# The values matmuls of half a head pair in one group, with the work of two other engines re-placed around it

## The chip, the cores and the metric

The kernel runs on one core of a Trainium2 chip. What counts is the device time of one launch in microseconds (us). The core has five engines that each run their own instructions in order: PE (TensorE, matmuls; its weight loads are listed apart as PEld), DVE (VectorE), ACT (ScalarE), POOL (GpSimd) and SP (SyncE, which issues most of the DMAs). They wait for each other by semaphores.

## The reference

The program is bucketed attention for 4 batches of 8 heads (768 positions, 64 channels a head), followed by a feed-forward layer with a rational function as its activation:

```python
mask = q_bucket[:, :, :, None] == k_bucket[:, :, None, :]   # bucket: the signs of 6 projections
scores = scale * np.matmul(q, k.transpose(0, 1, 3, 2))
scores = np.where(mask, scores, -1000000000.0)
scores = scores - np.max(scores, axis=-1, keepdims=True)
attn = np.exp(scores)
attn = attn / (np.sum(attn, axis=-1, keepdims=True) + 1e-09)
out = np.matmul(attn, v)
# then, on the tokens: h = x @ w_in;  g = P(h) / (Q(h) + 1e-6);  y = g @ w_out
```

All of it is in fp32. The fast matmul form takes numbers of fewer bits, so the kernel splits an operand into a rounded high part and the low rest, and multiplies the parts.

## The kernel before

**Attention, by head pairs.** Two heads make a pair, and there are 16 pairs. A pair has 12 steps `s`: two halves of the queries (`hf`, 384 columns each) by six tiles of 128 keys. One step is

- `scores`: for each of the two heads two matmuls (high parts with the mask rows, 76 or 77 rows deep; then the low parts, 128 deep) into one PSUM bank `pss`, and one Exp on ACT from that bank into an SBUF tile `E`; POOL adds the `E` tiles of three steps into an accumulator `acc` (two adds, one for each head, at each second and third step);
- `values`: for each head one matmul of `E` with the values `v` into the bank `psv` of that half, 64 columns of weights wide, the two heads beside each other. These are fp32 matmuls; each shows as two passes. After the sixth step `values_out` copies the bank out on ACT (`col`, then `xo`).

`sums` adds the accumulators over the partitions with eight narrow matmuls (32 columns of ones) into the bank `psu`, and ACT copies them to `sr`. So that Exp never overflows, each pair's largest scores are found beforehand: `maxstep` computes two matmuls into `psm` and DVE reduces them to a column of `m`, twelve times a pair, two pairs ahead. `shift_turn` turns the maxima by a matmul with the identity (`pst`, then `mt` on DVE).

**Preparation, beside it.** For a pair two ahead ACT rounds q and k to their high parts (`high`), DVE subtracts these from the originals (`low`, tiles `lo`), `bits` multiplies q and k with the projections (`psb`, 32 columns wide, for two pairs at once), DVE makes bucket rows `mb` of them, and ACT scales these (`penalties`). `weights` converts one of the 32 weight tiles every six steps, from 64-bit words: ACT takes both halves of a word (`ws`, `wr`), DVE masks, shifts and combines them (a TENSOR_SCALAR, a SCALAR_TENSOR_TENSOR and an add of integers, which the profile calls CUSTOM_DVE and the program order ISA), ACT rounds the result (`wi_hi`, or `wr` for w_out), and DVE subtracts (`wi_lo`, or `wr`). `recips` takes the reciprocals of the sums of a batch, after each fourth pair.

**What sets the order.** A plan by hand: `at(p, s, f)` puts the call `f` at time 12·p + s, and the calls are issued in the order of these numbers. Each engine keeps this order, so a number decides both which neighbours a call has on its engine and what stands behind it in the queue. Before, the values of a step are issued 1.3 to 2.3 steps after its scores, for two steps at a time (in pairs 0 and 15 for one), and `weights`, `low` and `high` stand at steps of their own among the scores. PSUM has eight banks: three rotate under the tag `s` (scores, transposes, sums), one holds `v`, and two double banks hold `psm` and `psb`. `E` has six buffers and `acc` six.

**After attention** come 128 steps of the feed-forward layer (`psh`, `pso`), from about 437 us to the end. All lines of the profile read L61, that of the helper that records the order; instructions are told apart by their tiles.

Of the kernel before, what the change touches and what calls it, by code (L numbers as in the profile page):

```python
# [17 lines left out]
P = 128  # L18
# [19 lines left out]
ACCS = 6  # L38
# [99 lines left out]
def attention(ctx, tc, nc, raw, ps_b, tail, tokens, early, operands_to_terms, ffn, load, QF, KF, v, w_in, w_out, wo_d, ident, cst, ones, prj,  # L138
# [15 lines left out]
    Q1, Q2, K1, K2, LO, V, M, MB, ACC, EXP, AV, MS = ({} for _ in range(12))  # L154
# [33 lines left out]
    def bits(p, which=(0, 1)):  # L188
# [5 lines left out]
        sl = slice(64 * which[0], 64 * which[-1] + 64)  # L194
# [31 lines left out]
    def shift_turn(p, hf=None):  # L226
# [4 lines left out]
        ps = ps_b.tile([P, 512], F32, tag="s", bufs=3, name=f"pst{p}_{hf}")  # L231
# [14 lines left out]
    def scores(p, s):  # L246
# [3 lines left out]
        for h in range(2):  # L250
            ps = ps_b.tile([P, 512], F32, tag="s", bufs=3, name=f"pss{p}_{s}_{h}")
# [31 lines left out]
    def sums(p):  # L283
        ps = ps_b.tile([P, 512], F32, tag="s", bufs=3, name=f"psu{p}")
# [33 lines left out]
    def weights(i):  # L318
# [13 lines left out]
        else:  # L332
# [34 lines left out]
    for p in range(NPAIR):  # L367
        for s in range(12):
# [17 lines left out]
        if p > 1:  # L386
            for t in range(2):
# [267 lines left out]
```

## Time and profile before

| what | value |
|---|---|
| median of 3 runs | 985.38 us (982.52 to 987.13) |
| the profiled execution | 982.12 us |
| its span, first to last instruction | 980.3 us |
| busy share of the span, PE / PEld / DVE / ACT / POOL | 98 / 76 / 85 / 69 / 45 % |
| attention, up to the first `psh` | about 437 us |

The page lists busy times, the span in 40 slices, the chain that ended last, and the costliest groups of instructions. In a row such as `PE MATMUL psv<-E,v 128*64 128x385` the tile written stands left of the arrow, the tiles read right of it, then the weights (rows*columns) and the streamed operand. In a timeline the columns are the start, the time from the first start to the last end, the engine, and how many instructions are merged; what is in brackets is the idle time before and what ended it.

### The profile page before, as it was taken

The page shows a single profiled execution, that of the slowest core. Times are in us where ns is not written, and L with a number is a line of the kernel's source. Part 1 is how long each engine was busy: PE and PEld are TensorE (multiplying, and loading weights), DVE is VectorE, ACT ScalarE, POOL GpSimd, SP SyncE. Part 2 cuts the span into 40 slices and gives each one's busy share as a digit, 9 for nine tenths or more (in the row PEclk, how much of TensorE's full clock was granted, in tenths as well). Part 3 has the DMA queues.
Part 4 walks back from the last instruction along what each step waited for, and adds up shares of the span by engine and source line. Part 5 has one row for each costly group of instructions (what it writes and reads, how often), then busy time and mean ns, then how long its engine had stood idle before and what let it go on. Part 6 is the DMA issues. An engine that isn't in the chain of part 4 may idle for free.

```text
span 980.3 us, 14803 instructions
## 1 busy us (share of the span) xinstructions
PE 957.6 (98%) x5009; PEld 744.8 (76%) x5009; DVE 835.4 (85%) x1200; ACT 679.2 (69%) x1411; POOL 436.8 (45%) x396
## 2 busy tenths in 40 slices
PE   5899999999999999999999999999999999999998
PEld 2556666666656666559999999999999999999996
DVE  5487778777877777568999999999999999999996
ACT  2356767676666666678777777777777777777775
POOL 1257776777677777782222222222222222222222
PEclk7699999999999999999999999999999999999999
DMA  7656676767686767737502111011011021110000
GB/s 202 175 169 185 184 201 171 202 186 198 183 254 211 242 190 206 236 126 260 169 1 66 33 49 48 1 65 33 1 65 33 1 65 33 62 36 1 33 1 32
DMA packets 50491, 112.97 MB, mean 115 GB/s; under 512 B 9296, under 2 KB 21968, under 8 KB 50416
## 3 DMA queue, kind: packets, MB, share of 16 engines
q1 hardware_dynamic: 49580, 110.59, 37.9%
q10 hardware_dynamic: 836, 1.44, 0.6%
q8 instruction: 39, 0.64, 0.3%
q14 instruction: 36, 0.29, 0.1%
HBM read 56.82 MB, written 21.17 MB: 80 GB/s over the span
## 4 chain that ended last, share of the span: by engine, by line
PE 92%; DVE 3%; DMA 3%; ACT 1%; SPq 0%; issue 0%; ACTq 0%; DVEq 0%
PE psh L61 27%; PE pso L61 27%; PE pss L61 15%; PE psv L61 13%; PE psm L61 6%; PE psu L61 2%; DVE m L61 1%; PE psb L61 1%; DMA wr<-w_out 1%; DMA q<-lo 0%; SPq L61 0%; DVE c L61 0%; DMA v<-v 0%; DMA prj<-proj 0%; DMA q<-mt 0%
## 5 line engine op out<-in xcount | busy, mean ns | idle before, releaser
L61 POOL TENSOR_TENSOR gl<-c,gh 128x384 fp32r<-128x384 f32 x128 | 140.4, 1097 | 395.4 <-ACT gh L61 368.8
L61 DVE TENSOR_REDUCE m<-psm 128x1 f32<-128x768 f32 x192 | 182.0, 952 | 92.5 <-PE psm L61 90.4
L61 PE MATMUL pso<-wo,gh 128*128 128x512 f32 x768 | 241.1, 395 | 0.0
L61 ACT ACTIVATE E<-pss 128x384 f32<-128x384 f32 x384 | 168.3, 492 | 79.7 <-PE pss L61 72.8
L61 POOL TENSOR_TENSOR acc<-E,E 128x384 f32<-128x384 f32 x128 | 150.9, 1199 | 113.9 <-ACT E L61 113.9
L61 PE MATMUL pss<-q,k 77*128 77x384 f32 (+1 forms) x768 | 180.2, 357 | 2.5 <-DMA q<-mt 1.5
L61 PEld LDWEIGHTS pss<-q,k 77*128 77x128 f32 (+1 forms) x768 | 134.0, 192 | 60.3 <-issue 50.1
L61 PE MATMUL psh<-xl,wi_hi 128*128 128x384 f32 x512 | 172.1, 336 | 0.0
L61 PE MATMUL psh<-xh,wi_hi 128*128 128x384 f32 x512 | 171.8, 336 | 0.0
L61 PE MATMUL psh<-xh,wi_lo 128*128 128x384 f32 x512 | 171.6, 335 | 0.0
L61 PEld LDWEIGHTS pso<-wo,gh 128*128 128x128 f32 x768 | 142.9, 188 | 23.7
L61 PE MATMUL pso<-wo,gl 128*128 128x512 f32 x384 | 152.3, 397 | 0.3 <-POOL gl L61 0.3
L61 ACT ACTIVATE h<-psh 128x384 f32<-128x384 f32 x128 | 62.9, 492 | 123.9 <-PE psh L61 123.9
L61 PE MATMUL psv<-E,v 128*64 128x385 f32 x768 | 148.3, 503 | 0.0
L61 DVE SCALAR_TENSOR_TENSOR c<-c,ab,r 128x384 f32<-128x384 f32 x128 | 146.9, 1147 | 0.0
L61 POOL TENSOR_TENSOR acc<-acc,E 128x384 f32<-128x384 f32 x128 | 142.7, 1135 | 7.8 <-ACT E L61 5.9
L61 PE MATMUL psm<-k,q 76*128 76x384 f32 x384 | 107.8, 365 | 7.0 <-DMA k<-mb 3.7
L61 PEld LDWEIGHTS psh<-xh,wi_hi 128*128 128x128 f32 x512 | 96.1, 188 | 6.3 <-ACT w L61 0.6
L61 PEld LDWEIGHTS psh<-xl,wi_hi 128*128 128x128 f32 x512 | 96.1, 188 | 5.1
L61 PEld LDWEIGHTS psh<-xh,wi_lo 128*128 128x128 f32 x512 | 96.2, 188 | 0.0
L61 PEld LDWEIGHTS psv<-E,v 128*64 128x64 f32 x768 | 45.7, 136 | 60.0 <-issue 52.4
L61 ACT ACTIVATE c<-psh,ab 128x384 f32<-128x384 f32 x128 | 86.5, 676 | 1.7 <-POOL gl L61 1.7
(62 smaller groups left out, 1233.8 us busy)
## 6 DMA issues: line engine op xcount, KB each, us to landing
q<-q SPq DMA_DIRECT2D x48, 192.0 KB
k<-k SPq DMA_DIRECT2D x48, 192.0 KB
wr<-w_in SPq DMA_DIRECT2D x16, 512.0 KB
wr<-w_out SPq DMA_DIRECT2D x16, 512.0 KB
wo_d<-wr SPq DMA_DIRECT2D x16, 512.0 KB
wo<-wo_d SPq DMA_DIRECT2D x16, 512.0 KB
q<-lo SPq DMA_DIRECT2D x32, 192.0 KB
k<-lo SPq DMA_DIRECT2D x32, 192.0 KB
```

Source lines behind the costliest of these rows:

```text
L61: return self.tc.keep_in_program_order(issue(*args, **kwargs))
```

## The change

- The values of a half are issued together: all twelve matmuls and `values_out` at step 6·hf + 6.3, that is, behind the scores of the first step of the next half. `sums` follows at 12.31, right behind the second group, and `bits` (for pairs above 2) at 0.32 of the next pair, behind the sums.
- `E` has seven buffers and `acc` five. The bank `v` is given up; `psv` and the feed-forward `psh` rotate with the others under `s`, which now has four banks.
- Right ahead of a group's number stand calls that read no values: `high` and `low` (0.25, 0.26) ahead of the second group, and of `weights` the mask, shift, combining and rounding (6.25 to 6.28) ahead of both. Their subtraction stands at 9.4, between two maxima.
- `sums` and its copy to `sr` are parted: `sr` is at 13.1, behind the next scores. `bits` and the DVE step that makes the rows (`bucket_rows`, 0.5) are parted as well; `penalties` are at 1.2 and `maskrows` at 2 or 4.
- `shift_turn` is at 6.9 and `shift_rows` at 8 (before 8 and 10), and the `recips` steps are at 16.5, 18.27 and 20 (before 20, 22 and 23).

```diff
-    E = [ep.tile([P, 2, HQ + 2], F32, name=f"E{i}") for i in range(6)]
+    E = [ep.tile([P, 2, HQ + 2], F32, name=f"E{i}") for i in range(7)]
...
+        PSB[p + which[0]] = ps
+
+    def bucket_rows(p, which=(0, 1)):
+        sl = slice(64 * which[0], 64 * which[-1] + 64)
+        ps, mb = PSB.pop(p + which[0]), MB[p + which[0]][0]
         nc.vector.tensor_scalar(out=mb[sl], in0=ps[sl, :, 0:HQ], scalar1=0.0, scalar2=cst[sl, 0:1], op0=ALU.is_gt, op1=ALU.subtract)
...
-            AV[p, hf] = ps_b.tile([P, 512], F32, tag="v", name=f"psv{p}_{hf}")
+            AV[p, hf] = ps_b.tile([P, 512], F32, tag="s", bufs=4, name=f"psv{p}_{hf}")
...
-        ACC[p] = tail.tile([P, HQ], F32, tag="sr", name=f"sr{p}")
-        nc.scalar.copy(ACC[p], ps[:, 0:HQ])
+        ACC[p] = ps
 
     def sums_store(p):
-        sr = ACC.pop(p)
+        sr = tail.tile([P, HQ], F32, tag="sr", name=f"sr{p}")
+        nc.scalar.copy(sr, ACC.pop(p)[:, 0:HQ])
...
             nc.scalar.activation(lw.bitcast(I32), lw.bitcast(U32), AF.Copy, scale=2.0 ** -29)
+            yield
             nc.vector.tensor_scalar(out=hw.bitcast(I32), in0=hw.bitcast(I32), scalar1=-(1 << 31), scalar2=None,
                                     op0=ALU.bitwise_and)
-            yield
...
-            if not 0 < p < NPAIR - 1:
-                at(p, s + 2.3, values, p, s)
-            elif s % 2:
-                at(p, s + 1.3, values, p, s - 1)
-                at(p, s + 1.3, values, p, s)
-            if s % NT == NT - 1:
-                at(p, s + (1.3 if 0 < p < NPAIR - 1 else 2.3), values_out, p, s // NT)
+        for hf in range(2):
+            for i in range(NT):
+                at(p, 6 * hf + 6.3, values, p, 6 * hf + i)
+            at(p, 6 * hf + 6.3, values_out, p, hf)
...
-            at(p, 14.5, sums, p)
-            at(p, 16, sums_store, p)
+            at(p, 12.31, sums, p)
+            at(p, 13.1, sums_store, p)
         if p > 1:
+            first = p == 2
+            if p % 2 == 0:
+                at(p - 2, 3 if first else 0.32, bits, p)
+                at(p - 2, 3 if first else 0.5, bucket_rows, p)
+                at(p - 2, 4 if first else 1.2, penalties, p)
             for t in range(2):
-                at(p - 2, t, high, p, t)
-                at(p - 2, 2 + t, low, p, t)
...
+                at(p - 2, t if first else 0.25, high, p, t)
+                at(p - 2, 2 + t if first else 0.26, low, p, t)
...
-            spread(p, (20, 22, 23), recips(p // NHP))
+            spread(p, (16.5, 18.27, 20), recips(p // NHP))
+
     for i in range(2 * NFC):
-        o = 6 * i - 3
-        late = (10.5, 12.5, 13.5, 14.5) if i < 2 * NFC - 1 else (10.5, 10.8, 11, 11.2)
-        spread(0, [o + x for x in (4, 7, 8, 9) + late], weights(i))
+        times = (1, 5.4, 6.25, 6.26, 6.28, 9.4, 11) if i < 2 * NFC - 2 else (1, 4, 5, 6, 6.5, 7.5, 8)
+        if i == 2 * NFC - 1:
+            times = (0.5, 3, 3.5, 4, 4.5, 5.5, 6.2)
+        spread(0, [6 * i + x for x in times], weights(i))
```

Where the change moves instructions is shown as rows of the program's order (operation, tile written<-tiles read, size; the last number in a name tells the tile, the one before it the step, or for `psv` the half). The place is the end of pair 5 and the beginning of pair 6.

On PE, before, around the second step of pair 6:

```order
L61 MATMUL psm_4_1942<-k_7_1722,q_7_1696 128x384 x2
L61 MATMUL pss_0_0_1947<-q_6_1404,k_6_1430 128x384
L61 MATMUL pss_0_0_1947<-q_6_1690,k_6_1691 128x384
L61 MATMUL pss_0_1_1951<-q_6_1404,k_6_1430 128x384
L61 MATMUL pss_0_1_1951<-q_6_1690,k_6_1691 128x384
L61 MATMUL psm_5_1955<-k_7_1722,q_7_1696 128x384 x2
L61 MATMUL psv_1_1890<-E_152,v_1519 64x385 x2
L61 MATMUL psv_1_1890<-E_153,v_1519 64x385 x2
L61 MATMUL pss_1_0_1976<-q_6_1404,k_6_1430 128x384
```

and now:

```order
L61 MATMUL psm_5_1946<-k_7_1689,q_7_1687 128x384 x2
L61 MATMUL psv_1_1968<-E_151,v_1520 64x385 x2
L61 MATMUL psv_1_1968<-E_152,v_1520 64x385 x2
L61 MATMUL psv_1_1968<-E_153,v_1520 64x385 x2
L61 MATMUL psv_1_1968<-E_154,v_1520 64x385 x2
L61 MATMUL psv_1_1968<-E_148,v_1520 64x385 x2
L61 MATMUL psv_1_1968<-E_149,v_1520 64x385 x2
L61 MATMUL psu_1985<-acc_0_0_1733,ones 32x384 x2
L61 MATMUL psu_1985<-acc_1_0_1867,ones 32x384 x2
L61 MATMUL psu_1985<-acc_0_1_1789,ones 32x384 x2
L61 MATMUL psu_1985<-acc_1_1_1915,ones 32x384 x2
L61 MATMUL psb_0_1995<-qf_1581,prj 32x384
```

Four values matmuls between the scores have become twelve, with the sums and the projections directly behind them.

On ACT, now, at the same place:

```order
L61 CAST q_8_1956<-qf_1581 128x768
L61 CAST k_8_1958<-kf_1583 128x768
L61 CAST wi_hi<-ws_1876 128x512
L61 COPY col_1_1981<-psv_1_1968 128x1
L61 ACTIVATE xo_1_1982<-psv_1_1968,col_1_1981 128x384
L61 ACTIVATE E_151<-pss_1_0_2005 128x384
L61 ACTIVATE E_151<-pss_1_1_2009 128x384
L61 COPY sr_2025<-psu_1985 128x384
L61 ACTIVATE mb_1994<-mb_1994,cst 128x768
L61 ACTIVATE E_152<-pss_2_0_2030 128x384
```

The rounding of q, of k and of the weights now stands ahead of the copies of the values (before, that of k and of the weights stood behind the next step's Exps), and the copy `sr` of the sums stands between the Exps of steps 1 and 2.

On DVE, before, one half later:

```order
L61 TENSOR_SCALAR wr_2149<-wr_2149 128x512
L61 TENSOR_REDUCE m_2144<-psm_4_2223 128x1
L61 SCALAR_TENSOR_TENSOR ws_2150<-ws_2150,wr_2149 128x512
L61 TENSOR_REDUCE m_2144<-psm_5_2236 128x1
L61 ISA ws_2150<-wr_2149,ws_2150 128x1024
L61 TENSOR_REDUCE m_2144<-psm_6_2268 128x1
L61 TENSOR_REDUCE m_2144<-psm_7_2288 128x1
L61 TENSOR_TENSOR lo_9_2292<-qf_1839,q_9_2246 128x768
```

and now:

```order
L61 TENSOR_SCALAR wr_2156<-wr_2156 128x512
L61 SCALAR_TENSOR_TENSOR ws_2157<-ws_2157,wr_2156 128x512
L61 TENSOR_TENSOR lo_9_2243<-qf_1851,q_9_2237 128x768
L61 TENSOR_TENSOR lo_9_2245<-kf_1853,k_9_2239 128x768
L61 ISA ws_2157<-wr_2156,ws_2157 128x1024
L61 TENSOR_REDUCE m_2151<-psm_6_2286 128x1
```

Five operations that were parted by the reductions of maxima now stand in one row; the reductions are left with one subtraction among six.

More of the change, by code (lines that the diff above doesn't have):

```diff
@@ L37 @@
 PARTS = 2
-ACCS = 6
+ACCS = 5
 TINY = 2.0 ** -80
@@ L149, in attention @@
     ps_a = ctx.enter_context(tc.tile_pool(name="ps_a", bufs=2, space=PSUM))
-    E = [ep.tile([P, 2, HQ + 2], F32, name=f"E{i}") for i in range(6)]
+    E = [ep.tile([P, 2, HQ + 2], F32, name=f"E{i}") for i in range(7)]
     for e in E:
         nc.gpsimd.memset(e[:, :, HQ : HQ + 2], TINY)
-    Q1, Q2, K1, K2, LO, V, M, MB, ACC, EXP, AV, MS = ({} for _ in range(12))
+    Q1, Q2, K1, K2, LO, V, M, MB, ACC, EXP, AV, MS, PSB = ({} for _ in range(13))
     def load_v(p, queue=nc.sync):
@@ L250, in scores @@
         for h in range(2):
-            ps = ps_b.tile([P, 512], F32, tag="s", bufs=3, name=f"pss{p}_{s}_{h}")
+            ps = ps_b.tile([P, 512], F32, tag="s", bufs=4, name=f"pss{p}_{s}_{h}")
             nc.tensor.matmul(ps[:, 0:HQ], K1[p][0:77, h, ks], Q1[p][0:77, h, qs], start=True, stop=False)
@@ L283, in sums @@
     def sums(p):
-        ps = ps_b.tile([P, 512], F32, tag="s", bufs=3, name=f"psu{p}")
+        ps = ps_b.tile([P, 512], F32, tag="s", bufs=4, name=f"psu{p}")
         for k in range(PARTS):
@@ L383, in attention @@
         if p < NPAIR - 1:
-            at(p, 14.5, sums, p)
-            at(p, 16, sums_store, p)
+            at(p, 12.31, sums, p)
+            at(p, 13.1, sums_store, p)
         if p > 1:
-            for t in range(2):
-                at(p - 2, t, high, p, t)
-                at(p - 2, 2 + t, low, p, t)
-            if p % 2 == 0:
-                at(p - 2, 3 if p == 2 else 2, bits, p)
-                at(p - 2, 4 if p == 2 else 3, penalties, p)
-            at(p - 2, 2, high_move, p)
-            at(p - 2, 6 if p == 2 else 4, maskrows, p)
+            first = p == 2
[3 more added lines that the diff above has]
+                at(p - 2, 4 if first else 1.2, penalties, p)
+            for t in range(2):
+                at(p - 2, t if first else 0.25, high, p, t)
+                at(p - 2, 2 + t if first else 0.26, low, p, t)
+            at(p - 2, 2 if first else 1, high_move, p)
+            at(p - 2, 6 if first else 2 if p % 2 == 0 else 4, maskrows, p)
         if p > 0:
@@ L421, in attention @@
     bits(0, (0,))
+    bucket_rows(0, (0,))
     penalties(0, (0,))
@@ L427, in attention @@
     bits(0, (1,))
+    bucket_rows(0, (1,))
     penalties(0, (1,))
@@ L465, in __call__ @@
     def __call__(self, t, f):
-        tag, bufs = (("s", 3), ("v", 1), ("s", 3), ("s", 3))[f % 4]
-        ps = self.out[t, f] = self.pool.tile([P, 512], F32, tag=tag, name=f"psh{t}_{f}", bufs=bufs)[:, 0:NTK]
+        ps = self.out[t, f] = self.pool.tile([P, 512], F32, tag="s", name=f"psh{t}_{f}", bufs=4)[:, 0:NTK]
         fs = slice(f * P, f * P + P)
```

10 lines of the change are left out of this document (4 added, 6 removed).

## The prediction, made before the change was run

> **What bounds the kernel now.** I read the page's busy shares first, then the stretches, then PE's timeline.
>
> ```profile
> span 980.3 us, 14803 instructions
> PE 957.6 (98%) x5009; PEld 744.8 (76%) x5009; DVE 835.4 (85%) x1200; ACT 679.2 (69%) x1411; POOL 436.8 (45%) x396
> ```
>
> ```profile
> 300.00:400.00 100.00, 99.36 (x572) 64.45 (x571) 75.86 (x97) 68.09 (x151) 73.12 (x64) 1.00 0.72 216
> 500.00:600.00 100.00, 100.00 (x503) 90.29 (x502) 97.69 (x150) 75.63 (x153) 25.78 (x24) 1.00 0.13 40
> ```
>
> The columns of a stretch are its length, the busy time of PE, PEld, DVE, ACT and POOL, the granted clock, the DMA share and GB/s. PE is full in both stages at full clock. The change touches only the first, up to 437 us; the feed-forward stage keeps its order and its four banks, so I count it as moved, not shortened. In attention DVE, ACT and POOL still have 24 to 32 us free of each 100: nothing but PE sets the pace there, so what counts is PE's own time and every wait that it is given.
>
> PE's time holds a cost that the busy share hides:
>
> ```profile
> 56.01 0.87 PE L61 MATMUL psv<-E,v 128*64 128x385 f32 x4
> 56.81 0.98 PE L61 MATMUL pss<-q,k 77*128 77x384 f32 x4
> ```
>
> ```profile
> 250.06 1.51 PE L61 MATMUL psv<-E,v 128*64 128x385 f32 x8
> 251.50 0.97 PE L61 MATMUL pss<-q,k 77*128 77x384 f32 x4
> 252.31 0.52 PE L61 MATMUL psm<-k,q 76*128 76x384 f32 x2
> 252.67 0.88 PE L61 MATMUL pss<-q,k 77*128 77x384 f32 x4
> 253.39 0.52 PE L61 MATMUL psm<-k,q 76*128 76x384 f32 x2
> 253.84 0.55 PE L61 MATMUL psv<-E,v 128*64 128x385 f32 x2
> ```
>
> From start to start, two `psm` take 0.36 us ahead of `pss` (252.31 to 252.67) and 0.45 ahead of `psv`: 0.09 more. Four `pss` take 0.72 behind `psm` and 0.81 behind `psv`: 0.09 more. Eight `psv` passes take 1.44, four take 0.80 (56.01 to 56.81), so four more cost 0.64, eight bare ones 1.28, and a group carries 0.16 whatever its length. **One visit to the narrow matmuls costs 0.34 us beside their work.**
>
> **What it removes.** In the order of PE I count the entries from wide matmuls (`pss`, `psm`, `psh`) into narrow ones (`psv`, `psu`, `psb`): 105 before, 34 with the change (two a pair, for the sums and projections now follow values, and two at the ends). 71 × 0.34 = 24.1 us. The number of matmuls is the same.
>
> It also moves the reciprocals of a batch beside a group. Before, they delayed a reduction that PE waited for:
>
> ```profile
> PE psm L61 <- DVE m L61: 2.0, 3, 0.7
> ```
>
> (From the table of waits of 60 to 430 us: the total, how often, the longest.) Three waits, 2.0 us: with a group of over 4 us on PE, DVE has the time. I count them all as gone. Together 26.1 us.
>
> **What it adds.** During a group no score and no maximum is computed, so ACT's Exps and DVE's reductions are squeezed into the six steps between groups. A step of PE is 0.72 + 0.36, so six are 6.4 us; a group is twelve matmuls of two passes, two beside each other, so 24 passes at 0.16 plus 0.34, some 4.2; the sums add 1.4:
>
> ```profile
> 246.30 1.50 PE L61 MATMUL psu<-acc,ones 128*32 128x384 f32 x16
> 247.73 0.98 PE L61 MATMUL pss<-q,k 77*128 77x384 f32 x4
> ```
>
> The projections of even pairs are as many passes again, 1.3. Now what the others do in that time:
>
> ```profile
> L61 DVE TENSOR_REDUCE m<-psm 128x1 f32<-128x768 f32 x167 | 158.7, 952 | 80.2 <-PE psm L61 78.2
> L61 DVE SCALAR_TENSOR_TENSOR ws<-ws,wr 128x512 int32<-128x512 int32 x30 | 22.6, 755 | 0.0
> L61 DVE CUSTOM_DVE_ANT_0 ws<-wr,ws 128x1024 uint16<-128x1024 uint16 x30 | 21.7, 723 | 0.3
> L61 DVE TENSOR_SCALAR wr<-wr 128x512 int32<-128x512 int32 x30 | 14.8, 495 | 10.1 <-ACT ws L61 10.1
> L61 DVE TENSOR_TENSOR lo<-kf,k 128x768 fp32r<-128x768 f32 x13 | 12.3, 949 | 0.0
> ```
>
> ```profile
> L61 ACT ACTIVATE E<-pss 128x384 f32<-128x384 f32 x356 | 155.6, 492 | 51.9 <-PE pss L61 45.6 <-POOL acc L61 2.3
> L61 ACT ACTIVATE xo<-psv,col 128x384 f32<-128x384 f32 x30 | 17.4, 581 | 1.0
> L61 ACT CAST wi_hi<-ws 128x512 fp32r<-128x512 f32 x15 | 9.5, 631 | 0.0
> L61 ACT COPY sr<-psu 128x384 f32<-128x384 f32 x15 | 7.2, 479 | 35.1 <-PE psu L61 35.1
> ```
>
> *(a) The copy of the sums, every pair.* ACT's first Exp after a group starts some 0.7 us after PE's first score (0.62 for two matmuls with the entry, and the hand-over); two Exps occupy 0.87 to their end; `sr` follows, 0.48, and ends at about 1.95. Its bank is the fourth that is asked for: PE wants it for the second head of the next step, at 0.81 + 0.36 + 0.36 = 1.5. PE waits 0.5. Behind it on PE stand that step's maxima and all later scores. Before, the copy was done with nothing else ahead of it: ACT sat waiting for `psu` (35.1 us). 15 × 0.5 = 7.5 us; bounds 0.3 and 0.8.
>
> *(b) The copies of the values, odd pairs.* On ACT `col` and `xo` now stand behind the rounding of the weights, which needs DVE's combining step, the last of five behind the last reduction. Counted from the group's start: last reduction 1.1; mask, shift, two `lo` and combine 0.4 + 0.7 + 0.9 + 0.9 + 0.6 = 3.5, so 4.6; rounding 0.6, `col` 0.2, `xo` 0.6: 6.0. PE asks for that bank at 4.2 + 1.3 + 1.2 = 6.7, so as it stands there is no wait. But POOL's adds come between:
>
> ```profile
> 149.55 0.95 DVE L61 TENSOR_TENSOR lo<-kf,k 128x768 fp32r<-128x768 f32 x1
> 150.42 1.50 DVE L61 TENSOR_TENSOR wi_lo<-ws,wi_hi 128x512 fp32r<-128x512 f32 x1
> ```
>
> ```profile
> 150.18 2.61 POOL L61 TENSOR_TENSOR acc<-E,E 128x384 f32<-128x384 f32 x2 [3.64 <-ACT E L61]
> ```
>
> ```profile
> L61 DVE TENSOR_TENSOR wi_lo<-ws,wi_hi x16: 670/684/1502, 59.4 to 250.8; 128x512 fp32r<-128x512 f32 x16
> ```
>
> The add issued at 150.18 ends only some 0.87 after DVE's `lo` (150.50), the subtraction at 150.42 only 0.55 after that add, and the second add after the subtraction, at 152.79. They take turns. With one or two adds of the half still due, the five end 0.9 to 1.8 later, and PE waits 0.2 to 1.1. Even pairs have the projections' 1.3 as cover. I take 0.6 × 7 = 4 us; bounds 0 and 8.
>
> The Trainium skill, "SBUF — State Buffer", section "SBUF: two separate sides", states that the port pair that DVE and GpSimd share is an exclusive lock held for a whole instruction, and that the other fully blocks. By that rule all five alternate with the adds, (b) is at its upper end and the sum 4 us worse; the mask and the shift show little of this in their means (495 and 755), so I keep the middle.
>
> *(c) The subtraction among the reductions, every half.* Six reductions at some 0.87 from start to start take 5.2 of the 6.4, and the subtraction adds 0.6 alone or 1.4 behind an add (684 at the median, 1502 at most). With the short one all fit; with the long one the fourth reduction ends late, and the sixth `psm`, which needs its bank, waits up to 0.6. 28 halves have one. POOL is busy most of that time, so about 40% take the long way: 28 × 0.23 = 6.5 us; bounds 0 and 17.
>
> *(d) The end.* Behind pair 14's first half there are no maxima, and PE needs 8.5 us a half. POOL's eight adds need more:
>
> ```profile
> 417.76 3.08 POOL L61 TENSOR_TENSOR acc<-E,E 128x384 f32<-128x384 f32 x2 [0.62 <-ACT E L61]
> 420.81 1.82 POOL L61 TENSOR_TENSOR acc<-acc,E 128x384 f32<-128x384 f32 x2
> ...
> 436.18 2.72 POOL L61 TENSOR_TENSOR acc<-acc,E 128x384 f32<-128x384 f32 x2
> ```
>
> Sixteen adds from 417.76 to 438.90, less 2.0 idle, are 1.2 us each with their waits, 9.5 a half. The last three halves run at POOL's pace: 3 us; bounds 0 and 6.
>
> ```profile
> L61 POOL TENSOR_TENSOR acc<-E,E 128x384 f32<-128x384 f32 x120 | 142.5, 1207 | 92.3 <-ACT E L61 92.3
> L61 POOL TENSOR_TENSOR acc<-acc,E 128x384 f32<-128x384 f32 x118 | 132.7, 1145 | 6.6 <-ACT E L61 4.7
> ```
>
> In the stretch of 60 to 430 us POOL's means are 1207 and 1145 ns, some 1.15 from start to start. The Exps themselves fit: twelve at 0.37 are 4.5 of 6.4. The seventh `E` lets the first step of the next half pass ahead of a group, and POOL's 16 adds (some 18 us a pair) fit into 23.5 to 24.5. The five `acc` suffice, for the sums now stand ahead of the next pair's first add.
>
> **The sum.** −26.1 + 7.5 + 4 + 6.5 + 3 = −5.1. The profiled execution, 980.3 of span and 982.1 in all, would become 977. It lies 3.3 under the median of the runs (985.4); against that median I predict **980 us**. With every bound low the sum is −21.6 (964), with every bound high (12 + 8 + 17 + 6) it is +17 (1002); both need all four to err together. The forecast's own range is 974 to 986.
>
> **Rivals.**
>
> *The cover holds.* If DVE and POOL rarely meet, (b) and (c) are nearly nothing and (d) small: −26.1 + 7.5 + 2 = −17, 969 us. For it: 684 at the median of the subtractions. Against: it needs POOL idle when DVE's row of operations starts, and POOL's work per half is 9 of 11 us.
>
> *DVE and POOL together become the bound; slower.* Per pair 16 adds of about 0.92 (1.82 for two without a meeting) are 14.7, and DVE's SBUF work is 2 × (0.4 + 0.7 + 0.7 + 0.7) + 1.9 = 6.9: 21.6 of 23.5 us, if they exclude each other. Should an add hold DVE off for 1.0 or more, it is 23, no slack is left, and every group ends with a wait for the last add or for the combining step, at 0.5 us a half more than I count: 28 × 0.4 = +11, 991 us. For it: POOL's means, well above 0.92. Against: most of that is the meeting itself.
>
> *Transfers come late.* The weights are asked for 4.4 steps before ACT needs them, now some 5 us.
>
> ```profile
> ACT ws L61 <- DMA wr<-w_out: 3.4, 4, 2.4
> ```
>
> Four of 30 were late already. If half of the 16 of w_out are late by 1.5 us, and a third of that passes through DVE to PE, it is +4: 984 us. Against: the wait falls into a group, which hides much of it. That the visits would not be saved at all cannot be: the order shows the groups whole.
>
> **How the numbers follow.** Forecast 0.5, the cover holds 0.2, DVE and POOL bound 0.2, late transfers 0.1. What a measurement here tells from no change is 0.5%, 4.9 us: faster is below 980.5, slower above 990.3. The forecast's 974 to 986 lies about half below 980.5 (0.25), the rest within; the cover gives 0.2 faster; the bound 0.05 within and 0.15 slower; late transfers 0.01 faster, 0.07 within and 0.02 slower. What may go wrong beyond these adds a little on the slow side. Faster 0.46, same 0.35, slower 0.19. The range 967 to 991 leaves out the ends of the two outer cases.
>
> **What would show it.** Right: twelve steps of `psv` passes in one row, entries at 34, attention some 5 us shorter; PE waits for `sr` in each pair, for `xo` in odd ones, and `psm` for `m` at the end of some halves. The forecast is wrong if PE in attention has no waits beyond 10 us in sum (the cover holds), or if the chain runs through POOL's adds for whole halves (the bound), or if ACT's waits for `wr` grow beyond 10 us (transfers).

## The result, and the profile after

The changed kernel takes **1027.7 us** (median of 4 runs, 1021.3 to 1031.6), against 984.3 for the kernel before on the same chip: a ratio of 1.043, with a 95% interval of 1.037 to 1.050. It is slower by 43 us, where 980 was predicted. Attention, up to the first `psh`, takes 476.4 us in place of 437.2; the feed-forward stage is as long as before.

The page of the kernel after the change; the last row is the granted clock in 40 slices, in tenths:

```profile
span 1019.5 us, 14799 instructions
...
PE 960.8 (94%) x5009; PEld 765.0 (75%) x5009; DVE 854.8 (84%) x1200; ACT 676.9 (66%) x1411; POOL 406.5 (40%) x397
...
PEclk8599997999899897999999999999999999999999
```

The same row of the kernel before:

```profile
PEclk7699999999999999999999999999999999999999
```

PE is busy for 94% of the span and not 98, and in four slices from the seventh to the sixteenth the clock is below 9 tenths. Before, no slice behind the second was. So there are two losses: PE stands still, and when it works it works in part at half clock. The waits of 60 to 430 us after the change name what it stands for (total, how often, the longest):

```profile
PE psm L61 <- DVE m L61: 15.6, 16, 3.9
...
PE pss L61 <- DMA q<-mt_None: 11.5, 7, 4.5
DVE rz L61 <- DMA rs<-s_d: 10.1, 3, 3.6
...
ACT ws L61 <- DMA wr<-w_out: 7.0, 3, 4.2
```

The same table of before had 2.0 us for `psm <- m` and no DMA that PE waits for. Two new things stand out: DVE's `rz`, the first step of the reciprocals, waits three times for the sums (`rs<-s_d`), and PE itself waits seven times for the transposed maxima (`q<-mt_None`).

**One of the three stops in the order of time.** First the DMA issues of SP in the timeline after the change (start, duration of the issue):

```profile
146.30 0.58 SPq L61 DMA_DIRECT2D wr<-w_in  x1
151.98 1.10 SPq L61 DMA_DIRECT2D s_d<-sr  x2
...
157.12 1.17 SPq L61 DMA_DIRECT2D q<-q  x2
...
161.15 0.45 SPq L61 DMA_DIRECT2D rs<-s_d  x1
```

SP issues nothing from 146.9 to 152.0: the store of the sums, `s_d<-sr`, is next in its queue, and ACT's copy of the sums ends only at 152.0. SP's own waits from 145 to 163 us say the same:

```profile
SPq L61 <- ACT sr L61: 5.0, 1, 5.0
```

The moves of the next pair (`q<-q`, which is `second_high`), the values and q and k all stand behind that store, and are issued in one burst up to 163. The stretches show what the DMA engines make of it (columns as in the prediction: the last three are the granted clock, the DMA share and GB/s):

```profile
152.00:156.00 4.00, 4.00 (x24) 3.81 (x23) 3.80 (x5) 4.00 (x10) 3.97 (x5) 1.00 0.12 21
...
160.00:164.00 4.00, 4.00 (x25) 2.96 (x21) 0.74 (x2) 2.84 (x7) 1.34 (x2) 1.00 1.01 263
164.00:168.00 4.00, 0.31 (x2) 0.00 (x0) 3.80 (x7) 0.87 (x2) 2.41 (x3) 0.73 0.85 277
168.00:172.00 4.00, 3.75 (x12) 3.75 (x13) 3.40 (x5) 1.13 (x3) 1.44 (x2) 0.50 0.20 64
172.00:176.00 4.00, 4.00 (x14) 3.05 (x14) 2.08 (x4) 3.85 (x8) 2.46 (x3) 0.50 0.57 143
```

The DMA engines are nearly idle (0.12) and then full (1.01), and the 24 KB of `rs` are asked for in the full stretch. DVE and PE in the same time:

```profile
164.09 0.59 DVE L61 TENSOR_SCALAR rz<-rs 128x48 f32<-128x48 f32 x1 [3.21 <-DMA rs<-s_d]
...
167.12 0.21 DVE L61 TENSOR_SCALAR mt_None<-pst_None 12x128 fp32r<-12x128 f32 x1
```

```profile
163.45 0.86 PE L61 MATMUL pss<-q,k 77*128 77x384 f32 x4
168.25 1.01 PE L61 MATMUL psm<-k,q 76*128 76x384 f32 x2 [3.94 <-DVE m L61]
169.06 1.49 PE L61 MATMUL pss<-q,k 77*128 77x384 f32 x4
```

`rs` lands at 164.1, DVE's five steps, `mt` and the reductions stand behind it, and PE waits 3.94 us. The stretch of 164 to 168 has a clock of 0.73, those up to 176 one of 0.50: four `pss` take 1.49 from first start to last end in place of 0.86. In the records the half clock lasts 10.2 us. The other two ends of a batch look the same.

**The row of maxima.** Issue and first use of `q<-mt_None`, after the change, and then the issue of a pair before it (whose first score starts at 140.64, in the same timeline):

```profile
110.45 0.81 SPq L61 DMA_DIRECT2D q<-mt_None  x1
```

```profile
116.39 0.94 PE L61 MATMUL pss<-q,k 77*128 77x384 f32 x4 [1.62 <-DMA q<-mt_None]
```

```profile
131.79 0.78 SPq L61 DMA_DIRECT2D q<-mt_None  x1
```

Before, 8.9 us lay between the issue and the first score that needs the row. After, PE asks for it at 114.8, 4.3 us behind the issue. The row is made no later in the plan, but the five steps between the transpose of the maxima and the next pair's first score now hold no values: from the one to the other it was 9.5 us before (131.1 to 140.6), and is 5.6 with the change (109.2 to 114.8).

**A ledger of PE.** I added up PE's timeline from start to start, from the first `psu` to the first `psh`, and split it in three: intervals above 0.45 us (0.8 at half clock), less the pass itself, are stops; of the intervals in the records' half clock the part that full clock would have saved (0.177 in place of 0.32 a pass) is the clock's; the rest is passes at full clock, entries and small waits included. In us, of the profiled executions, with the median of all runs and the ratio to the kernel before (95% interval):

| kernel | passes | stops | half clock | sum | median | ratio |
|---|---|---|---|---|---|---|
| before | 363.3 | 3.7 | 0 | 367.0 | 984 | |
| after | 345.9 | 42.8 | 18.5 | 407.2 | 1027.7 | 1.037–1.050 |
| reciprocals later | 345.6 | 42.4 | 15.0 | 403.0 | 1015.0 | 1.028–1.038 |
| stops filled | 356.4 | 38.8 | 15.5 | 410.7 | 1017.2 | 1.030–1.036 |
| transfers earlier | 348.5 | 24.6 | 4.4 | 377.6 | 990.3 | 1.002–1.009 |
| both | 347.7 | 32.1 | 6.3 | 386.0 | 1003.0 | 1.015–1.023 |
| subtraction in the group | 347.3 | 19.3 | 1.4 | 368.0 | 986.2 | 1.001–1.005 |
| copies first | 347.8 | 21.8 | 0 | 369.6 | 990.3 | 1.000–1.007 |
| all three | 346.8 | 24.9 | 9.5 | 381.2 | 998.6 | 1.009–1.021 |
| all three, store in place | 346.0 | 11.3 | 1.8 | 359.1 | **969.8** | 0.984–0.988 |
| second weight too | 344.3 | 18.1 | 15.1 | 377.4 | 986.8 | 1.001–1.007 |
| before, with a stop | 364.0 | 17.6 | 9.9 | 391.6 | 1008.2 | 1.023–1.029 |

So the groups do save PE's time, 17 us in passes. The change then adds 39 us of stops and 18.5 of half clock. (A profiled execution is one of several: that of the change is its fastest, 1021.3, that of the kernel with the stops filled its slowest, 1023.9. Compare medians for the time and the split for the cause.)

### The profile page after: what moved, and what is told of

It reads as the page before. It is cut to its first block, busy times and chain, and to the rows that moved or that the text cites. A ratio compares the mean times of both kernels' runs of the same rounds, so it can differ in the third digit from the quotient of the medians.

```text
span 1019.5 us, 14799 instructions
## 1 busy us (share of the span) xinstructions
PE 960.8 (94%) x5009; PEld 765.0 (75%) x5009; DVE 854.8 (84%) x1200; ACT 676.9 (66%) x1411; POOL 406.5 (40%) x397
## 4 chain that ended last, share of the span: by engine, by line
PE 78%; DMA 9%; DVE 8%; SPq 3%; issue 1%; ACT 1%; POOL 0%; DVEq 0%; ACTq 0%
PE psh L61 26%; PE pso L61 26%; PE psv L61 9%; PE pss L61 8%; PE psm L61 5%; DVE m L61 4%; SPq L61 3%; DMA q<-mt_None 3%; PE psu L61 2%; DMA k<-mb 2%; DMA k<-lo 1%; DVE wi_lo L61 1%; DMA rs<-s_d 1%; DVE wr L61 1%; PE psb L61 1%
## 5 line engine op out<-in xcount | busy, mean ns | idle before, releaser
L61 DVE TENSOR_REDUCE m<-psm 128x1 f32<-128x768 f32 x192 | 178.4, 951 | 72.1 <-PE psm L61 66.8
L61 ACT ACTIVATE E<-pss 128x384 f32<-128x384 f32 x384 | 166.2, 497 | 73.6 <-PE pss L61 67.7
L61 POOL TENSOR_TENSOR acc<-E,E 128x384 f32<-128x384 f32 x128 | 139.7, 1111 | 188.3 <-ACT E L61 188.0
L61 PE MATMUL pss<-q,k 77*128 77x384 f32 (+1 forms) x768 | 180.9, 362 | 18.7 <-DMA q<-mt_None 11.5
L61 PEld LDWEIGHTS pss<-q,k 77*128 77x128 f32 (+1 forms) x768 | 141.9, 201 | 36.6 <-issue 16.1
L61 PE MATMUL psv<-E,v 128*64 128x385 f32 x768 | 142.4, 522 | 2.0 <-ACT E L61 2.0
L61 PE MATMUL psm<-k,q 76*128 76x384 f32 x384 | 111.6, 378 | 22.7 <-DVE m L61 18.4
L61 POOL TENSOR_TENSOR acc<-acc,E 128x384 f32<-128x384 f32 x128 | 125.7, 1002 | 1.7 <-ACT E L61 1.5
L61 PEld LDWEIGHTS psv<-E,v 128*64 128x64 f32 x768 | 55.6, 146 | 76.3 <-issue 66.0
L61 PEld LDWEIGHTS psm<-k,q 76*128 76x128 f32 x384 | 74.6, 209 | 37.1 <-DVE m L61 27.2
```

The lines of the kernel that those rows point to most:

```text
L61: return self.tc.keep_in_program_order(issue(*args, **kwargs))
```

## The experiments

**The reciprocals later.** In the changed kernel:

```diff
-            spread(p, (16.5, 18.27, 20), recips(p // NHP))
+            spread(p, (16.5, 21.5, 23), recips(p // NHP))
```

> Three pairs (those of the fourth, eighth and twelfth step of the pair loop) begin with a stop of 3.9 us of PE, because the subtraction of the maxima's row waits on DVE behind `rz`, and `rz` for a load of the sums that lands late. Behind each stop the trace shows about 10 us at half the granted clock. Here the reciprocals' three steps stand five and three steps later, nothing else is changed. Theory 1 (the late load stops DVE, DVE stops PE, and the stop costs the clock): the three waits of 3.9 us go, and so do the 10.2 us of half clock behind each; 3 x (3.9 + 5.1) = 27 us less, about 1000 us by the median of 1027.7; the three pairs take 24 to 25.5 us in place of 32 to 33.6. Theory 2 (DVE and POOL together are the bound, and the waits only show where that work queues): the work is the same, the time stays within 5 us of the change.

1015.0 us: 13 less, half of what theory 1 expected and more than theory 2 allows. The waits of 60 to 430 us say why:

```profile
PE pss L61 <- DMA q<-mt_None: 21.5, 10, 5.1
PE psm L61 <- DVE m L61: 5.0, 15, 0.7
```

The three stops behind DVE are gone (15.6 to 5.0), but those for the row of maxima have grown from 11.5 to 21.5. While PE waited for the sums, the late transfers had time to land; without that wait they are the next to be late. This points to SP's queue behind both; the run after the next tests it.

**The stops filled.** Twenty more matmuls whose result nobody reads, at the place of the three stops:

```diff
+    def fill(p):
+        ps = ps_b.tile([P, 512], F32, tag="s", bufs=4, name=f"psf{p}")
+        for i in range(20):
+            nc.tensor.matmul(ps[:, 0:HQ], K1[p][0:77, 0, 0:P], Q1[p][0:77, 0, 0:HQ], start=True, stop=True)
...
+        if p in (4, 8, 12):
+            at(p, 9, fill, p)
```

> The change with twenty matmuls more in each of those three pairs (the shape of a score, their result is read by nobody), put where PE stands still for 3.9 us: the program does more, in time that is lost anyway. Twenty take 20 x 0.18 = 3.6 us. Theory 1 (the stop of PE itself makes the granted clock fall, and half of the loss is the clock): the three stretches at half clock go, 3 x 5.1 = 15 us less than the change, about 1012 us, though the waits' cause stays. Theory 2 (the clock falls for another reason, or it costs nothing because other engines set the pace): no gain, 1028 us, or up to 3 us more.

1017.2 us, 10.5 less with more work. In its timeline, and in the stretches (columns as above), the same place:

```profile
166.93 3.64 PE L61 MATMUL psf<-q,k 77*128 77x384 f32 x20
171.05 0.62 PE L61 MATMUL psm<-k,q 76*128 76x384 f32 x2 [0.49 <-DVE m L61]
```

```profile
168.00:172.00 4.00, 3.51 (x20) 3.19 (x19) 3.90 (x8) 0.00 (x0) 1.22 (x2) 1.00 0.66 244
```

DVE is as late as before, but PE is busy, and the clock stays at 1.00. So the half clock follows from PE's standing still, and costs time of its own. It did not bring the whole 15 us, for half clock stands at other places: 6.8 us each with waits of some 3 us for the row of maxima at 227 and 337 (that at 337 was there before the filling), and 10.2 us behind one of 1.2 us for `xo` at 403.

**The transfers earlier.** Only the order on SP:

```diff
-            at(p - 1, 3, second_high, p)
-            at(p - 1, 4, load_v, p)
+            at(p - 1, 0, second_high, p)
+            at(p - 1, 4 if p == 1 else 1.05, load_v, p)
...
-            at(p - 1, 9.6 if p == 1 else 8, shift_rows, p)
+            at(p - 1, 9.6 if p == 1 else 6.95, shift_rows, p)
...
-            at(p - 4, 6.5, load, p)
+            at(p - 4, 6.5 if p == 4 else 1.07, load, p)
```

> The change with another order on the DMA queues of SP alone: the moves and loads for the next pair are asked for at the first steps of a pair, when SP's queue stands idle, and the move of the row of maxima goes ahead of the weights' load; no work of PE, DVE, ACT or POOL is moved. Theory 1 (the transfers stand behind a burst of others in SP's queue and land 1.2 to 4.5 us late): seven waits of PE for the row of maxima, 11.5 us in sum, go, and with them the half clock behind them, some 4 us: about 1012 us. The three stops by the reciprocals stay. Theory 2 (DVE and POOL are the bound): within 5 us of 1028.

990.3 us: 37 of the 43 us are gone, more than expected, since the reciprocals' three stops went as well. The moves and loads now stand ahead of the store that waits for the sums. The stretches from 148 us on, the same pair as above:

```profile
148.00:152.00 4.00, 4.00 (x24) 3.82 (x23) 3.81 (x5) 4.00 (x11) 3.96 (x5) 1.00 1.00 360
152.00:156.00 4.00, 3.72 (x23) 1.72 (x23) 3.97 (x5) 1.78 (x4) 3.58 (x4) 1.00 0.37 101
156.00:160.00 4.00, 4.00 (x26) 2.92 (x23) 3.33 (x10) 2.85 (x7) 1.25 (x2) 1.00 0.01 3
```

The full stretch of the DMA engines has ended before `rs` and the maxima are asked for. The loads, the moves and the place of the row itself were changed in one, so what each of them gave is not shown. What is left of PE's waits of 60 to 430 us:

```profile
PE psm L61 <- DVE m L61: 8.6, 21, 0.8
PE pss L61 <- ACT xo L61: 5.8, 8, 1.3
...
PE pss L61 <- DMA q<-mt_None: 0.6, 1, 0.6
```

The first two rows are the prediction's terms (c) and (b). With these left the kernel is still 0.2 to 0.9% slower than the one before the change.

**Both**, the reciprocals later and the transfers earlier:

> The reciprocals later and the transfers earlier, both as in the two kernels before. Theory 1: the two gains add up, -27 and -15: about 985 us; pairs from sums to sums near 24.5 us, no granted clock under 0.98 in 60 to 440 us. What the grouping itself does to the time could be read from this one: the first prediction's own terms would make it 977 to 980. Theory 2 (DVE and POOL bound): no less than 1015.

1003.0 us, 13 worse than the transfers alone. The group of DVE that is the first of the five steps, from 60 to 430 us, with the transfers alone and then with both:

```profile
L61 DVE TENSOR_SCALAR rz<-rs 128x48 f32<-128x48 f32 x3 | 0.6, 184 | 0.1
```

```profile
L61 DVE TENSOR_SCALAR rz<-rs 128x48 f32<-128x48 f32 x3 | 2.8, 943 | 0.0
```

In the group, where POOL has no add, the step takes 0.18 us; among the reductions, where POOL adds, 0.94. Three of the five steps grow so, the reductions behind them are late by over 2 us, and PE stops for 3.3 to 4.0 us again, with half clock behind. So the change was right to put the reciprocals beside a group, and my expectation was wrong.

**The subtraction in the next group**, on top of the earlier transfers, for the first sixteen pieces (the sixth time of `weights`, and the end of the generator):

```diff
-        times = (1, 5.4, 6.25, 6.26, 6.28, 9.4, 11) if i < 2 * NFC - 2 else (1, 4, 5, 6, 6.5, 7.5, 8)
+        times = (1, 5.4, 6.25, 6.26, 6.28, 12.27 if i < 16 else 9.4, 12.28 if i < 16 else 11) if i < 2 * NFC - 2 else (1, 4, 5, 6, 6.5, 7.5, 8)
```

> The kernel with the earlier transfers (990.3 us), and for the sixteen pieces of the first weight the subtraction `wi_lo` taken from among the reductions of a half and put behind the combining step of the next group. With the earlier transfers PE's sixth `psm` of nearly every half waits 0.55 us, and the subtraction takes 1.3 to 1.4 there. Theory 1 (the subtraction among the reductions costs 0.55 us in every half with one, as it always meets POOL's adds): sixteen halves less 0.55 are 8 to 9 us, about 981.5; no such wait in 50 to 235 us, and the subtraction takes 0.68 in its new place, where POOL has no add. Theory 2 (the reductions fall behind in any case, six of them at 0.87 with POOL's adds beside them): less than 3 us.

986.2 us, 4 less. The groups of DVE from 60 to 235 us, with the transfers alone and with the subtraction moved:

```profile
L61 DVE TENSOR_TENSOR wi_lo<-ws,wi_hi 128x512 fp32r<-128x512 f32 x13 | 17.3, 1330 | 0.0
```

```profile
L61 DVE TENSOR_TENSOR wi_lo<-ws,wi_hi 128x512 fp32r<-128x512 f32 x14 | 9.5, 680 | 0.0
```

It takes 0.68 where POOL has no add, as theory 1 said, and `psm <- m` falls from 8.6 to 2.8 us. The waits for `xo` rise from 5.8 to 8.1. In the ledger the stops are down by 5.3 and the half clock by 3.0. The profiled execution took 976.8 at a mean clock of 0.984, another one 987.7 at 0.971: with stops of 1.1 to 1.9 us left, how often the clock falls differs from run to run, and the median keeps less than the profile shows. The intervals of the two kernels overlap (1.001 to 1.005, 1.002 to 1.009): by the medians alone the 4 us are not clear of the noise; that the waits are gone the trace shows.

**The copies first**, on top of the earlier transfers: on ACT the rounding of the weights behind the copy of the values (6.28 to 6.35), and `sums_store`, the copy with its store, at 12.32 in place of 13.1.

> The kernel with the earlier transfers (990.3 us), and on ACT the copies of the values ahead of the rounding of the weights, the copy of the sums ahead of the first Exps; DVE and SP are not touched. Theory 1 (terms (a) and (b): PE waits for these copies): the waits for `xo`, 7.4 us in sum from 60 to 440 us, and some 0.1 to 0.3 us in each pair for `sr` go: 8 to 11 us, about 981; ACT's rounding of the weights then stands in front of the first Exps and may give 1 to 2 us back. The stretch of 10 us at half clock from 323.5 us on, which began with a wait of 1.3 us for `xo`, goes too if that wait caused it (5 us more, 976). Theory 2 (the bound is DVE with POOL, ACT only waits with them): the waits come back at `psm <- m`, no gain over 2 us.

990.3 us, no gain, and yet not by theory 2: the waits for `xo` are gone, but PE now waits 5.2 us for `q<-mb`. The expectation says that SP is not touched; but the store moved with the copy, and with it SP's order. **All three** edits together show the same more plainly, in the next run.

> The earlier transfers, the subtraction in the next group for the sixteen pieces of the first weight, and the copies ahead of the rounding. Theory 1 (these waits are all that stands between the change and what it removes): 990.3 less 8.5, 9 and 5 is 968 us; pairs of 23.6 to 24.2 us up to 235 us. Theory 2 (each wait removed comes back as another, since DVE and POOL have no time left): 983 or more.

998.6 us. Its SP issues in one pair, with the store of the sums now a step earlier:

```profile
135.68 1.42 SPq L61 DMA_DIRECT2D k<-k  x2
139.35 1.09 SPq L61 DMA_DIRECT2D s_d<-sr  x2
140.49 0.50 SPq L61 DMA_DIRECT2D q<-q  x1
```

SP stands from 137.1 to 139.4 with the store that waits for the sums, and the move of the high parts, the loads and the bucket rows are late behind it. I had moved the store along with the copy and was caught by what the change itself had done.

**All three, the store in its place.** The copy alone goes ahead:

```diff
-            at(p, 13.1, sums_store, p)
+            at(p, 12.32, sums_copy, p)
+            at(p, 13.1, sums_store, p)
```

> As the kernel with all three edits (998.6 us), but the store of the sums is asked for where it stood with the earlier transfers alone; only the copy stays ahead. In the kernel with all three the store stood ahead of the moves of the next pair in SP's queue and waited there for the sums: `q<-mb` was late by 0.8 to 1.5 us in five pairs, the sums of a batch were late twice, and two stops of 3.0 and 4.5 us brought 10.2 us of half clock each. Theory 1 (the order in SP's queue did it, and the three edits are good): those waits and both half-clock stretches go, 998.6 less 20 to 30: 968 to 978 us, faster than before the change. Theory 2 (DVE and POOL have no time left, the waits only move): 985 or more, with waits for `m` in their place.

969.8 us, 1.4% under the kernel before (0.984 to 0.988). SP in the same pair, and PE's largest waits of 60 to 430 us:

```profile
140.02 0.91 SPq L61 DMA_DIRECT2D q<-q  x1
...
144.33 1.12 SPq L61 DMA_DIRECT2D s_d<-sr  x2
```

```profile
PE psm L61 <- DVE m L61: 2.4, 8, 0.4
PE pss L61 <- ACT E L61: 1.9, 7, 0.6
```

No wait of these 370 us is above 1.1 us. From one pair's sums to the next, from the second pair up to 233 us, it is 22.7 to 24.3 us, against 24.1 to 25.6 before. DVE, ACT and POOL do all that they did, so theory 2 (no time left on DVE and POOL) falls.

**The second weight too**: its subtraction and store at 6.36 and 8.5, ahead of the first reduction of a half.

> As the kernel before it, and for the pieces of the second weight (from 235 us on) the subtraction stands ahead of the first reduction of a half and not among its reductions, its store earlier on SP. Theory 1: fourteen halves less 0.55, and no other wait: 6 to 8 us under the kernel before it, 962 to 970 us. Theory 2: the first reduction starts later by the subtraction's 0.7 and the wait returns at the sixth `psm`: no gain over 2 us.

986.8 us, worse by 17. DVE at the start of an even pair:

```profile
280.87 0.96 DVE L61 TENSOR_TENSOR lo<-qf,q 128x768 fp32r<-128x768 f32 x1 [1.93 <-DMA q<-lo]
282.45 0.96 DVE L61 TENSOR_TENSOR lo<-kf,k 128x768 fp32r<-128x768 f32 x1 [0.62 <-DMA k<-lo]
...
284.70 0.69 DVE L61 TENSOR_TENSOR wr<-ws,wr 128x512 fp32r<-128x512 f32 x1 [0.69 <-ACT wr L61]
285.30 1.01 DVE L61 TENSOR_SCALAR mb<-psb,cst 128x768 fp32r<-128x768 f32 x1
```

The subtraction waits for ACT's rounding and holds off the bucket rows, whose bank PE needs: PE stops for it by up to 2.0 us. But DVE's row was late before that: `lo` had waited 1.93 and 0.62 us for the moves `q<-lo` and `k<-lo`, and the edit had moved a store on SP as well. How much is owed to which stays open. Three stretches of 10.2 us at half clock follow, one of them behind a wait of 1.1 us for an Exp. Neither theory had this: where a gain of 6 to 8 us was expected, 17 were lost.

**The kernel before with the earlier transfers** (`second_high` at 0, `load_v` at 1.05, `load` at 1.07):

> The kernel before the change with the earlier moves and loads (the first parts of the next pair's operands at steps 0 and 1), nothing else. Theory 1 (the transfers are late only because a group leaves six short steps between the last maximum of a pair and its first score; before the change they had 6 us of slack): no change, 983 +- 3. Theory 2 (SP's order was a cost before as well): 5 us or more faster.

1039.5 us (1.055 to 1.059): a miss for both theories. Its SP issues, DVE's subtraction for k, and PE's waits:

```profile
98.45 0.39 SPq L61 DMA_DIRECT2D qf<-qT  x1
103.54 0.33 SPq L61 DMA_DIRECT2D kf<-kT  x1
```

```profile
102.53 0.95 DVE L61 TENSOR_TENSOR lo<-kf,k 128x768 fp32r<-128x768 f32 x1
```

```profile
PE psm L61 <- DMA k<-mb: 33.1, 11, 3.9
```

The load of `kf` overwrites what DVE's `lo<-kf,k` still has to read; in the kernel before that stands among the reductions and starts at 102.5. SP waits for it from 98.8 to 103.5, and the bucket rows behind are late in eleven pairs. The earlier order is open only because the change does the rounding and the low parts beside a group, at the pair's start. Whether before had any cost from SP's order stays open.

**The kernel before, with a stop.** Eleven additions on DVE in pairs 4, 8 and 12, whose result nobody reads:

```diff
+    def stop(p):
+        for i in range(11):
+            nc.vector.tensor_tensor(out=idle, in0=idle, in1=idle, op=ALU.add)
...
+        if p in (4, 8, 12):
+            at(p, 3, stop, p)
```

> The kernel before the change with eleven additions on DVE (128 x 384, result read by nobody) among the reductions of pairs 4, 8 and 12, so that PE stands still there for some 4 to 6 us. It measures a stop by itself, without groups and without late transfers. Theory 1 (a stop of PE brings a stretch of half clock after it): three stretches under full clock within 3 us behind the stops, each 7 to 10 us long; the time rises by the stops and another 3 x 4, so by 25 to 30 us, 1008 to 1013. Theory 2 (the half clock of the changed kernel comes from something else): by the stops alone, 12 to 18 us, 995 to 1001.

1008.2 us, as theory 1 said. One stop in PE's timeline and in the stretches:

```profile
157.34 1.01 PE L61 MATMUL psm<-k,q 76*128 76x384 f32 x2 [4.36 <-DVE m L61]
```

```profile
152.00:156.00 4.00, 0.98 (x6) 0.66 (x4) 3.90 (x4) 1.44 (x3) 4.00 (x4) 0.83 0.25 79
156.00:160.00 4.00, 2.62 (x7) 2.11 (x8) 4.00 (x7) 0.77 (x2) 0.00 (x0) 0.50 0.04 10
```

The three pairs take 33.3, 33.6 and 33.1 us from sums to sums in place of 25.0: 8.1 to 8.5 more for a stop of 4.5 from start to start. **A stop of this length cost nearly twice its wait here**; the rest is half clock.

**Without the groups.** The values by twos of steps again, with their own bank, and all else as with the earlier transfers:

> The kernel with the earlier transfers without its groups: the values of a pair stand by twos of steps as before the change, with their own bank and three banks for the rest, and the sums two steps later; what the change moved on ACT, DVE and SP stays where the change put it. So 105 entries into narrow matmuls in place of 34. Theory 1 (an entry costs 0.34 us, whatever stands beside it): PE has 24 us more to do; the waits for the subtraction and the copies shrink, since reductions and Exps are not squeezed, some 15 us: about 1000 us, in which DVE's row of operations, now among the reductions, may cost up to 10 us more. Theory 2 (entries cost nothing beside the waits that they bring): about 980.

1110.4 us, far from both theories. It does not measure an entry:

```profile
136.23 0.62 ACT L61 CAST wi_hi<-ws 128x512 fp32r<-128x512 f32 x1 [3.75 <-DVE ws L61]
```

The rounding of the weights stands on ACT ahead of the Exps and waits for DVE's row of operations. Beside a group that is free; without one PE waits for the Exps, 48.0 us in 60 to 430. So the groups and the row of work beside them can't be tried apart in this way. What an entry costs can be read from PE's start-to-start times instead: at the median a bare wide pass takes 0.177 us, the interval from a wide matmul into a narrow one 0.268, and the one from a narrow into a wide one 0.417, in this kernel as in those before and after the change.

## Why the prediction was wrong

What failed is the account of what the change adds: it followed the engines' work beside a group, but not the transfers through SP's queue ("I count them all as gone", and a rival with one transfer), and it priced a wait of PE at its own length, without the clock. The runs showed 18 us of stops by late transfers and 18.5 us of half clock in place of −2.0 and nothing. By its own steps:

- **What PE's entries cost.** 34 entries, as counted (before, the trace has 107, not 105). In the ledger's stretch there are 63 fewer, which at 0.34 are 21.4 us, and the passes shrink by 17.4. In the best kernel, which has least else in it (346.0), 76 intervals between wide matmuls are of 0.2 to 0.3 us where its 31 returns from narrow ones explain 31; the other 45 lie 0.08 above a bare pass and look like small waits, some 3.6 us, against 25 such before. The intervals into and out of narrow matmuls are the same in every kernel (above). So the price was about right, and a part of what it saves is given back in waits too short to be listed.
- **The reciprocals, "I count them all as gone": this step failed.** The step looked at DVE's time beside a group and not at the load that the step waits for. In place of −2.0 came three stops of 3.9 us. The load is issued by SP, and the step had not been followed through SP's queue.
- **Transfers.** The rival "transfers come late" was there, but with one transfer only, `wr`, priced at +4 and with a chance of 0.1. The waits for `wr` came out at 7.0 and 3.2 us on ACT, just past the 10 us named as a sign, but hardly reached PE. The transfers that PE does wait for, the row of maxima above all, were not looked at. Both facts were to be had from the program order and the trace of before: the store of the sums had moved ahead of `second_high` on SP, and the 8.9 us from the issue of `q<-mt` to its use would shrink with the steps. Earlier transfers alone take the stops from 42.8 to 24.6: 18 us.
- **The clock.** The prediction noted a clock of 1.00 and took it as given. 18.5 us of half clock came with the stops. No term, bound or rival had it, and the range ended at 991.
- **(a), the copy of the sums**, 7.5: not seen. PE waits for `sr` in no row. The copy ends when the prediction said, 1.97 us after the first score of the pair shown above, but PE does not need its bank there: the second head of the next step starts at 151.52, while the copy runs from 151.47 to 151.96, and it is so in every pair.
- **(b), the copies of the values**, 4, bounds 0 and 8: with the earlier transfers 7.1 us from start to start, near the upper bound, but only in part by the turns with POOL's adds. Of the five operations the shift takes 1234 ns in the mean after 755 before, and the mask 620 after 495; the other three are as long as before (1009, 956 and 708 after 1022, 949 and 723). Ahead of the four longest waits for `xo` `lo` stood still for 0.3 to 1.3 us, for the moves `q<-lo` and `k<-lo`; over 60 to 430 us that is 9.6 us of DVE, and before the change there was none. So late transfers are in this term too. The rule of the Trainium skill that the prediction weighed ("SBUF — State Buffer", section "SBUF: two separate sides": an exclusive lock held for a whole instruction) put (b) at its upper end; the number is there, but that all five take turns is not what the trace shows. The reciprocals agree with it in three of their five steps, 0.2 us in a group and 0.9 beside the adds; of the other two one stays at 0.17 and the last at 0.45.
- **(c), the subtraction**, 6.5, bounds 0 and 17: one wait of 0.85 and 19 of 0.42 to 0.60 from start to start, 11.0 us in all. Not 40% of the subtractions take the long way but 21 of 29 (1.27 us and more): 13 of 15 for the first weight and 8 of 14 for the second.
- **(d), the end**, 3: from the fourteenth sums to the first `psh` the best kernel takes 46.4 us, before 39.7; 4.5 of the 6.7 is that the sums stand 2.2 steps earlier in the pair (an estimate, from some 2 us a step). That leaves some 2. The waits that the trace has there are two of 0.9 us for an Exp, and 3.4 us are at half clock; that POOL's pace is their cause is not shown.

So the four terms were 21 in sum and came out at 20, but by luck: 7.5 too much in (a) stands against 3 and 4.5 too little in (b) and (c). With −2.0 from the reciprocals they are 19 us of stops, and with the earlier transfers the stops are 20.9 above before. For the change as made, what was wrong is what is not among them: predicted −5, found +40 in the ledger. Of the 45 between, 18 are late transfers, 18.5 the half clock, 7 that the passes shrink by 17 and not by 24, and 2 the rest.

Most of the loss is a matter of SP's queue, but the sign is not settled by it alone: with the earlier transfers the ledger is still 10.6 us above before (passes −14.8, stops +20.9, half clock +4.4), not 5 below. Only with the subtraction and the copies re-placed as well is the kernel 1.4% faster than before. That is more than the 5 us that were forecast, but of a kernel from which most of (b) and (c) has been taken, so it does not bear out the forecast's sum. The rival "DVE and POOL together become the bound" is excluded by the same run.

## What to carry to other kernels

Where a change makes the steps of a plan shorter, everything that stands a fixed number of steps ahead of its use has less time: work out again for every transfer the time from issue to first use, not only for the large ones. A DMA queue is an engine with its own order: a store that waits for a result holds every load and move behind it, and what is then issued in one burst makes the small transfer late that is needed first. And price a stop of PE with the clock that comes with it before moving anything that can cause one: stops of some 4 us cost nearly twice their wait in the kernel with the additions, and about one and a half times with both edits (11.2 us of stops, 6.3 of half clock).

## What the runs showed of the hardware

In the kernel before with a stop, the granted clock fell to 0.50 some 2 to 5 us after the start of each stop of 4.5 us and stayed there for 6.8 to 10.2 us, though PE was busy through most of it. In all these traces the stretches at half clock between 60 us and the end of attention are near 3.4 us or two or three times that. The Trainium skill, "TensorE: Matmul & The Clock Gate", section "HAM oscillation — how this bites in real kernels", says that idle gaps above some 3.4 us bring PE back to half clock. The stops of 4 us agree. But with the earlier transfers a wait of only 1.15 us at 322.6 was also followed by 10.2 us at half clock, while one of 1.34 us at 272.5 in the same execution was not, nor was one of 2.0 us in the kernel with the copies first. Measured here, the length of one gap does not decide alone; what else does stays open.

Three of DVE's five steps on 128 x 48 numbers take 0.18 to 0.21 us in a group, where POOL has no add, and 0.9 among the reductions, where POOL adds. So how long such small work takes can be decided by where it stands.
